# Chunk attention and a token mixer on one core: two heads on alternate partitions, pair-writing transposes, three v buffers and another order

## The chip, the cores and the metric

The kernel runs on one core of a Trainium2 chip. The metric is device time in microseconds (us) from one launch; the runs before the change took 118.61 to 119.23 us, median 118.85. The engines are TensorE (PE, with its weight loads as PEld), VectorE (DVE), ScalarE (ACT), GpSimd (POOL) and SyncE (SP). Each engine runs its own instructions in order and waits on semaphores for the others.

## The reference

Two steps follow each other. First an attention in which each chunk of 64 tokens sees only itself; then a mixer over all 576 tokens of a batch. There are 8 batches, 8 heads, 576 tokens (9 chunks of 64) and 64 values per head.

```
scores = q_c @ k_c^T / sqrt(64)            # per batch, head, chunk: 64 x 64
attn   = exp(scores - max) / sum           # softmax over the chunk
x      = attn @ v_c                        # then heads side by side: [8, 576, 512]
W      = (x @ w_q) @ (x @ w_k)^T / sqrt(64)   # 576 x 576 per batch
out    = relu(W @ x) @ w_out               # [8, 576, 512], float32
```

The inputs are float32 and the output is float32. The kernel works in f16 with float32 sums in PSUM.

## The kernel before, in words

The whole program is one list of words, ORDER (lines 18 to 51). Each word is one step of one batch, and the loop at line 404 emits the steps in that order, so the list fixes the order of the instructions on every engine. `SC3.1@4` is a step SC of batch 3, part 1, into PSUM bank 4; `:A`, `:D` or `:P` at the end of a word says whether ScalarE, VectorE or GpSimd does it. A word that issues DMAs or has no letter has a fixed engine. The words, in the order in which a batch needs them:

- LD (`load`, line 115): a DMA issued by GpSimd that also turns float32 into f16. k and q come in two halves, `LD3.k0` and `LD3.k1`, each half holding four heads; v comes in four parts. Of v only half is loaded, in rows of two tokens; CP (`pair`, line 144) copies it within vt so that each row holds both members of a pair. vt has NVB = 4 buffers (line 81), used by batch number modulo 4, so a v load waits for the PV of four batches before.
- TR (`tr`, line 172): VectorE transposes 32 x 32 blocks of qk, seen as pairs of f16 in one float32, into kN or qT. One instruction covers one half (four heads) of k or of q: 576 elements in each partition. Each element is written 36 bytes (kN) or 72 bytes (qT) after the one before.
- MK (`mk`, line 182): copies kN into kT times a mask of zeros and ones, so that two heads that share a matmul don't mix. One word is two instructions, for even and for odd chunks.
- SC (`sc`, line 192): score matmuls on TensorE, 64 x 64 each, two at a time in the two halves of the rows. EX (line 206): the exponential, PSUM to SBUF, ScalarE. PV (line 220): attn times v, with a column of ones that gives the sum. RN (line 251): reciprocal and division on VectorE, into xn.
- XT, XE (lines 262, 270): transposing xn on TensorE and copying it out of PSUM. PJ, EP (lines 277, 299): the projection by w_q and w_k, copied into wqk. DU (line 302) copies half of it to the other partitions. WT, EW (lines 305, 313): the transposed w_k side. GM, EG (lines 320, 334): the product of w_k side and xn, 64 x 512, copied into g16. So W @ x is never formed from W; w_q side times g16 (MX, line 337) gives it. RL (line 349): relu, into rmx.
- OM, OE (lines 374, 386): the output projection for 128 rows, four matmuls of 512 columns, and its copy out of PSUM into the qk tile of that pair of batches, which is free by then. There are 36 of them. When a group of OE is complete, SyncE stores it. The first two stores are made to wait for the last two loads (line 476).
- ZZ (line 400): a dummy matmul of 512 columns on zeros, whose result nobody reads. There are 48, 41 of them before the first EP.

Other single words: CL (ones in vt), CZ (zeros in zz and wqk), MM (the mask), ID (identity), WS and WO (the weights).

GpSimd does the load issues and most CP and some DU words in one queue. A CP waits until its part of v has landed, and the loads behind it in the list wait with it.

The last lines of ORDER before, from the EP of batch 7 on, show how the end is built: eight output projections stand behind it.

```
MX6.0@0 OM24@6 RL6.0:A XT7.0@0 XT7.1@4 MX6.2@2 OM25@1 RL6.2:A XE7.0:D XE7.1:D PJ7@4 OM28@0 OE25:A EP7:A WT7@1 OM27@4
EW7:D GM7@1 OM29@5 OE29:D DU7:P OE28:A OE26:A OE24:A EG7:A OE27:A MX7.0@0 MX7.1@6 MX7.2@2 RL7.1:A RL7.0:D OM30@4
RL7.2:A MX7.3@6 RL7.3:A OE30:D OM31@0 OE31:D OM32@6 OM34@7 OM33@0 OE32:D OE34:A OE33:D OM35@7 OE35:A
```

Of the kernel before, what the change touches and what calls it, by code (L numbers as in the profile page):

```python
# [18 lines left out]
CZ ZZ@0 LD0.k0 MM ZZ@1 ZZ@2 ZZ@3 ZZ@4 ZZ@5 ZZ@6 ZZ@7 CL0 TR0.1 CL2 CL1 ZZ@0 ZZ@1 ZZ@2 LD0.q0 LD0.k1 LD0.q1 LD0.v1  # L19
LD0.v0 LD0.v2 LD0.v3 LD1.q0 LD1.v1 LD1.k0 ID WS LD2.q0 CP0.3:P LD1.k1 LD1.q1 CP1.1:P LD1.v0 LD1.v2 LD2.k0 LD1.v3 WO  # L20
LD2.v1 LD2.k1 CP1.0:P CP1.2:P LD2.v0 LD2.q1 CP1.3:P LD2.v2 LD2.v3 LD3.q0 TR0.0 TR0.3 MK0.3:D TR0.2 CP0.1:D CP0.2:D
MK0.0:A MK0.1:A MK0.2:A ZZ@3 ZZ@4 ZZ@5 ZZ@6 ZZ@7 ZZ@0 ZZ@1 SC0.0@0 ZZ@2 ZZ@3 ZZ@4 ZZ@5 ZZ@6 ZZ@7 SC0.2@6 SC0.1@4 EX0.0
CP0.0:A EX0.2 EX0.1 ZZ@2 PV0.0@2 ZZ@0 PV0.1@4 PV0.2@0 ZZ@6 ZZ@7 ZZ@6 ZZ@7 ZZ@6 RN0.0 RN0.1 ZZ@2 ZZ@3 ZZ@7 XT0.0@7 ZZ@6
XE0.0:A RN0.2 XT0.1@0 XE0.1:A ZZ@4 ZZ@5 ZZ@2 ZZ@3 ZZ@6 ZZ@4 PJ0@0 EP0:A TR1.1 TR1.0 MK1.0:D MK1.1:D SC1.0@4 WT0@0
EX1.0 TR1.3 EW0:D TR2.0 CL3 DU0:D TR1.2 MK1.2:A GM0@0 ZZ@7 ZZ@2 PV1.0@2 RN1.0 EG0:A MX0.2@0 MX0.3@6 MK1.3:A RL0.2:A
RL0.3:A TR2.1 MK2.1:D SC1.1@4 EX1.1 SC1.2@0 MX0.0@6 RL0.0:A ZZ@2 ZZ@3 ZZ@2 MX0.1@2 EX1.2 RL0.1:A PV1.1@4 PV1.2@0 ZZ@6
RN1.1 MK2.0:A OM1@6 XT1.0@7 RN1.2 OM2@4 XT1.1@0 XE1.0:D TR2.3 MK2.2:D MK2.3:D TR2.2 LD3.k0 LD3.k1 CP2.0:P LD3.v0
LD3.v1 LD4.k0 CP2.2:P LD3.q1 LD3.v2 LD4.k1 LD3.v3 CP3.0:P CP3.1:P LD4.v0 LD4.q1 LD4.q0 LD5.k0 CP3.2:P LD4.v2 LD4.v1
CP3.3:P SC2.0@2 OM0@7 OE1:A CP2.1:A XE1.1:A EX2.0 OE2:A PJ1@0 PV2.0@2 RN2.0 CP2.3:D TR3.0 EP1:A WT1@6 SC2.1@0 SC2.2@4
DU1:A EW1:A EX2.1 GM1@6 PV2.1@0 RN2.1 EX2.2 EG1:A OE0:A MX1.0@4 MX1.1@2 RL1.0:A RL1.1:A MX1.3@6 PV2.2@4 MX1.2@0  # L30
RL1.3:A RL1.2:A TR3.1 RN2.2 OM4@2 OM6@3 XT2.0@0 MK3.0:A XT2.1@4 TR3.3 MK3.1:D MK3.3:D MK3.2:D TR4.1 ZZ@6 TR3.2 OM5@1
SC3.0@6 OE4:A XE2.0:A XE2.1:A OE5:A EX3.0 PJ2@4 EP2:A OE6:A OM8@1 WT2@0 SC3.1@4 SC3.2@2 OE8:A EW2:A EX3.1 PV3.0@6
EX3.2 GM2@0 PV3.1@4 EG2:A MK4.1:A MK4.0:D TR4.3 RN3.0 OM7@2 OE7:A RN3.1 DU2:P LD5.q0 CP4.0:P LD4.v3 PV3.2@6 MX2.2@0
RL2.2:A MX2.1@4 RL2.1:A MK4.2:D RN3.2 TR4.0 MK4.3:D TR5.1 TR4.2 XT3.0@3 XE3.0:A MX2.0@0 OM3@2 RL2.0:A MX2.3@6 RL2.3:A
XT3.1@4 XE3.1:A LD5.q1 LD5.v1 LD5.k1 LD6.q0 LD5.v3 CP4.1:P CP4.2:P LD5.v0 CP4.3:P LD5.v2 CP5.1:P LD6.k0 LD6.v1 LD6.v3
LD6.k1 LD7.v0 LD6.v2 LD6.q1 LD6.v0 CP5.0:P CP5.2:P CP5.3:P LD7.k0 SC4.0@0 OM9@3 PJ3@4 EX4.0 OE9:A EP3:A OE3:A PV4.0@0
SC4.1@6 EX4.1 WT3@4 OM10@5 SC4.2@2 EW3:A EX4.2 MK5.0:D TR5.0 DU3:D RN4.0 PV4.1@6 RN4.1 GM3@4 PV4.2@0 RN4.2 OM11@2
MK5.1:A EG3:A OE10:A MX3.0@6 MX3.1@3 XT4.0@5 OE11:A RL3.0:A RL3.1:A XT4.1@0 SC5.0@6 MX3.2@2 TR5.3 XE4.0:D MK5.3:D
MK5.2:D TR5.2 XE4.1:A OM13@4 RL3.2:A EX5.0 PJ4@0 MX3.3@2 OM12@5 EP4:A RL3.3:A OE13:A OE12:A SC5.1@0 EX5.1 SC5.2@2
WT4@4 PV5.0@6 EX5.2 EW4:A TR6.0 TR6.1 RN5.0 OM16@5 PV5.1@0 RN5.1 PV5.2@2 GM4@4 RN5.2 OM15@6 XT5.0@7 OE16:A MK6.0:A  # L40
EG4:A MK6.1:D TR6.3 XE5.0:D TR6.2 MK6.3:D MK6.2:D TR7.1 LD7.k1 CP6.1:P LD7.q0 DU4:P LD7.v2 CP7.0:P LD7.v3 CP6.0:P
CP6.3:P LD7.q1 LD7.v1 CP6.2:P MX4.3@4 MX4.1@0 OE15:A RL4.3:A RL4.1:A XT5.1@2 XE5.1:A SC6.0@4 MX4.2@0 OM17@6 EX6.0
PJ5@2 OM14@7 MX4.0@4 OE17:A EP5:A RL4.2:A RL4.0:A WT5@6 EW5:D SC6.1@2 EX6.1 PV6.0@0 SC6.2@4 EX6.2 RN6.0 GM5@6 PV6.1@2
PV6.2@4 RN6.1 RN6.2 DU5:P EG5:A OE14:A MX5.0@0 OM19@6 OM20@7 MK7.1:A RL5.0:A OE19:A OE20:A XT6.0@2 XE6.0:A XT6.1@4
MX5.1@0 RL5.1:A MX5.2@6 TR7.3 XE6.1:D OM18@3 PJ6@4 MK7.3:A EP6:A RL5.2:A OM23@2 TR7.0 MK7.0:D SC7.0@0 WT6@4 MX5.3@6
OE18:A EW6:A CP7.2:P CP7.3:P CP7.1:P DU6:P TR7.2 OE23:D RL5.3:D MK7.2:D EX7.0 OM21@5 GM6@4 PV7.0@0 SC7.2@6 SC7.1@2
OE21:A EG6:A EX7.2 EX7.1 RN7.0 MX6.1@4 OM22@6 RL6.1:D MX6.3@0 PV7.1@2 PV7.2@4 RN7.1 RN7.2 RL6.3:A OE22:A OM26@7
MX6.0@0 OM24@6 RL6.0:A XT7.0@0 XT7.1@4 MX6.2@2 OM25@1 RL6.2:A XE7.0:D XE7.1:D PJ7@4 OM28@0 OE25:A EP7:A WT7@1 OM27@4
# [6 lines left out]
def kernel(  # L55
# [87 lines left out]

    def pair(b, half, f, eng):
        m = slice(NG // 2 * half, NG // 2 * (half + 1))
# [24 lines left out]
            )  # L170

    def tr(b, g, s):
        to = (kN if s else qT[b % 2])[:, g].bitcast(F32).rearrange("p n o -> p (n o)")
# [6 lines left out]
        nc.vector.transpose(out=to, in_=frm)  # L180

    def mk(b, g, hp, eng):
        one = mask[:, hp : hp + 1]
        for odd in range(2):
            dst = kT[b % 2][:, g, odd::2, hp ^ odd].rearrange("p c (e i) o -> p c e (i o)", e=2)
            frm = kN[:, g].rearrange("p (e c i) o -> p c e (i o)", e=2, c=NCH)[:, odd::2]
            if eng == "A":
                nc.scalar.activation(dst, frm, AF.Copy, scale=one)  # L188
            else:
                nc.vector.tensor_scalar(dst, frm, one, None, op0=ALU.mult)  # L190

    def sc(b, u, bank):
        for i in range(8 if u < 2 else 2):
            g, c = (u, i) if u < 2 else (i, NCH - 1)
            for e in range(2):
                for t in range(2):
                    rows = slice(CH * t, CH * t + CH)
                    nc.tensor.matmul(  # L198
                        ps[:, bank + t, CH * i : CH * i + CH],
                        lhsT=kT[b % 2][rows, g, c, :, :, e].rearrange("p f n -> p (f n)"),  # L200
                        rhs=qT[b % 2][rows, g, CH * c : CH * c + CH, e],
                        start=(e == 0),
                        stop=(e == 1),
                    )
# [199 lines left out]
    for word in ORDER:  # L404
# [17 lines left out]
        elif kind == "CZ":  # L422
            nc.vector.memset(zz[:].bitcast(F32), 0.0)  # L423
# [88 lines left out]
```

## Time and profile before

| | |
|---|---|
| median of 3 runs | 118.85 us (118.61 to 119.23) |
| the profiled execution, its own time | 118.47 us |
| its span, first to last instruction | 116.6 us |
| TensorE clock granted, mean | 0.985 of full |
| busy: PE, DVE, ACT, POOL | 99.8, 92.4, 89.5, 61.9 us |
| loads (GpSimd's queue), written | 14.82 MB |
| stores (SyncE's queue) | 9.44 MB |

All durations come from one execution, whose span is 116.6 us. A row of the slices gives for each fortieth of the span (2.9 us) the busy share of an engine in tenths, where 9 means 90% or more. In the groups, a row names line, engine, operation, what is written from what, the shape and the count, then the busy time in us and the mean of one in ns, then the idle time of the engine just ahead of such instructions and what ended it. In the view by windows a row is one stretch of time with the busy time of each engine in it and the number of its instructions. The chain of work that ended last follows the end of the span back to what released each step.

### The profile page before, as it was taken

The numbers are of one execution on the slowest core, as the hardware profiler recorded it, in microseconds if no ns is written. First come the engines' busy times: TensorE is split into PE (matmuls) and PEld (weight loads), VectorE is DVE, ScalarE is ACT, GpSimd is POOL, SyncE is SP. The second block draws the span as 40 slices with busy tenths as digits, with TensorE's granted clock in tenths as the row PEclk, the third lists the DMA queues.
The fourth block names the chain that finished last, engine by engine and source line by source line (L and its number), as shares of the span: only waits on it lengthen the run. The fifth ranks groups of instructions, "written<-read, shape, count | busy, mean of one in ns | idle before, by whom it ended". The sixth has DMA issues, their size and how long they took to land.

```text
span 116.6 us, 4132 instructions
## 1 busy us (share of the span) xinstructions
PE 99.8 (86%) x1768; PEld 55.9 (48%) x1768; DVE 92.4 (79%) x155; ACT 89.5 (77%) x142; POOL 61.9 (53%) x105
## 2 busy tenths in 40 slices
...
DVE  2099399999999999999997999998799768515520
...
PEclk9999599999999999999999999999999999999999
DMA  1999999999999999999999999999799986007982
GB/s 11 177 200 177 199 194 211 192 201 203 197 193 204 196 201 186 190 195 194 189 195 165 169 178 200 210 192 129 296 400 415 411 351 280 23 3 304 379 315 88
DMA packets 27202, 24.52 MB, mean 210 GB/s; under 512 B 20784, under 2 KB 20784, under 8 KB 27184
## 3 DMA queue, kind: packets, MB, share of 16 engines
q0 software_dynamic: 24880, 14.82, 90.8%
q1 hardware_dynamic: 2304, 9.44, 20.3%
q8 instruction: 14, 0.23, 0.7%
...
HBM read 29.62 MB, written 9.44 MB: 335 GB/s over the span
## 4 chain that ended last, share of the span: by engine, by line
DMA 43%; PE 33%; POOL 12%; issue 5%; ACT 2%; DVE 1%; POOLq 0%; DVEq 0%
DMA vt<-in_v_dram 39%; PE pb L378 18%; POOL vt L295 6%; DMA qk<-in_q_dram 4%; POOL vt L122 3%; POOL qk L138 3%; PE pb L341 3%; PE pb L198 3%; PE pb L283 3%; PE pb L266 3%; PE pb L325 2%; PE pb L232 2%; ACT qk L293 1%; DVE xn L255 1%; ACT rmx L356 1%
## 5 line engine op out<-in xcount | busy, mean ns | idle before, releaser
L378 PE MATMUL pb<-wout,rmx 128*128 128x512 f16 x144 | 36.4, 382 | 0.0
L255 DVE TENSOR_TENSOR xn<-pb,rec 128x896 f16<-128x896 f32 (+1 forms) x24 | 25.1, 1047 | 0.8
L295 POOL COPY vt<-vt 32x576 int32<-32x576 int32 x27 | 18.1, 674 | 11.4 <-DMA vt<-in_v_dram 10.7
L122 POOL DMA_DIRECT2D vt<-in_v_dram x32 | 21.8, 687 | 3.4 <-DMA vt<-in_v_dram 1.2
L356 ACT ACTIVATE rmx<-pb 128x576 f16<-128x576 f32 x29 | 18.3, 663 | 5.9 <-PE pb L341 5.7
L180 DVE STREAM_TRANSPOSE kN<-qk 128x576 f32<-128x576 f32 x16 | 19.4, 1213 | 4.0 <-DMA qk<-in_k_dram 4.0
L188 ACT ACTIVATE kT<-kN,mask 128x640 f16<-128x640 f16 (+1 forms) x24 | 17.4, 786 | 5.1 <-DVE kN L180 4.9
L293 ACT COPY qk<-pb 128x512 f32<-128x512 f32 x30 | 17.6, 607 | 4.1 <-PE pb L378 3.9
L180 DVE STREAM_TRANSPOSE qT<-qk 128x576 f32<-128x576 f32 x16 | 19.7, 1243 | 0.1
L208 ACT ACTIVATE est<-pb 128x1024 f16<-128x1024 f32 (+1 forms) x24 | 19.2, 826 | 0.4 <-PE pb L198 0.3
L378 PEld LDWEIGHTS <-rmx 128*128 128x128 f16 x144 | 12.5, 103 | 13.0 <-issue 0.5
L198 PE MATMUL pb<-qT,kT 64*128 64x64 f16 x576 | 13.0, 193 | 4.0 <-ACT kT L188 2.8
L401 PE MATMUL pb<-zz 128*128 128x512 f16 x48 | 14.5, 437 | 1.2 <-DVE zz L423 1.2
L190 DVE TENSOR_SCALAR kT<-kN,mask 128x640 f16<-128x640 f16 (+1 forms) x40 | 14.9, 423 | 0.1
L198 PEld LDWEIGHTS <-kT 64*128 64x128 f16 x576 | 10.8, 96 | 8.1 <-ACT kT L188 4.2
L293 ACT COPY xT<-pb 128x1280 f16<-128x1280 f16 (+1 forms) x10 | 11.4, 1146 | 4.0 <-PE pb L266 3.7
L295 POOL COPY wq<-wqk 64x288 int32<-64x288 int32 x5 | 2.1, 422 | 22.6 <-ACT wqk L293 19.1
L232 PE MATMUL pb<-vt,est 64*64 64x65 f16 x576 | 9.9, 197 | 2.4 <-issue 1.8
L266 PE MATMUL pb<-ident,xn 128*128 128x128 f16 (+1 forms) x160 | 10.9, 214 | 0.4 <-DVE xn L255 0.4
L266 PEld LDWEIGHTS <-xn 128*128 128x128 f16 (+1 forms) x160 | 9.2, 97 | 3.9 <-issue 1.2
L232 PEld LDWEIGHTS <-est 64*64 64x64 f16 x576 | 7.8, 109 | 6.4 <-issue 5.0
L138 POOL DMA_DIRECT2D qk<-in_k_dram x16 | 9.2, 576 | 2.5 <-DMA qk<-in_k_dram 1.1
...
## 6 DMA issues: line engine op xcount, KB each, us to landing
...
qk<-in_k_dram POOLq DMA_DIRECT2D x16, 288.0 KB, 8.0
qk<-in_q_dram POOLq DMA_DIRECT2D x16, 288.0 KB, 7.9
vt<-in_v_dram POOLq DMA_DIRECT2D x32, 144.0 KB, 7.8
...
```

The lines of the kernel that those rows point to most:

```text
L122: nc.gpsimd.dma_start(vt[b % NVB][CH * f + 32 : CH * f + CH, m, 0 : 2 * D], src[:, NG * half + f : NG * (half + 1) : 2],)
L180: nc.vector.transpose(out=to, in_=frm)
L188: nc.scalar.activation(dst, frm, AF.Copy, scale=one)
L198: nc.tensor.matmul(ps[:, bank + t, CH * i : CH * i + CH], lhsT=kT[b % 2][rows, g, c, :, :, e].rearrange("p f n -> p (f n)"), rhs=qT[b % 2] ...
L208: nc.scalar.activation(est[b % 2][u].rearrange("p i n c -> p i (n c)"), ps[:, bank : bank + 2, 0:n], AF.Exp, scale=scale_attn,)
L232: nc.tensor.matmul(ps[CH * o : CH * o + CH, bank + hp, VP * m : VP * m + VP], lhsT=est[b % 2][t][rows, i, at], rhs=vt[b % NVB][rows, slot, ...
L255: nc.vector.tensor_tensor(out=xn[b % 2][:, 7 * u : 7 * u + n].rearrange("p m (h d) -> p h m d", h=2), in0=xw[:, :, :, 0:D], in1=rec[u][:, ...
L266: nc.tensor.transpose(t16[:, at % 1024 : at % 1024 + r], xn[b % 2][0:r, n, :], ident[0:r, 0:r])
L293: nc.scalar.copy(dst, src)
L295: nc.gpsimd.tensor_copy(dst.bitcast(I32), src.bitcast(I32))
L356: nc.scalar.activation(dst, src, AF.Relu, scale=scale_moe)
L378: nc.tensor.matmul(ps[:, bank, :], lhsT=c.rearrange("p (t r) -> p r t", r=size)[:, r], rhs=wout[:, i, :], start=(i == 0), stop=(i == NI - 1),)
```

## The change

The two transposes of a batch's halves become one, for batches 1 to 7. Batch 0 keeps the old layout. For the others, a load of one half puts its 64 rows on every other partition, so that the two halves alternate from partition to partition; one row is 9216 bytes in memory, 36 tokens, where it was 4608 bytes. A transpose of all 128 partitions then finds the two halves side by side in each 32 x 32 block, and writes them side by side: two float32 of 4 bytes in a row, then a step. One TR instruction has 1152 elements.

The tiles follow: in kT and qT the two halves alternate element by element (8 bytes from one to the next of a half, as SC reads them), kN and kT get a tenth, empty chunk so that even and odd chunks fit one pattern, and one MK word is one instruction. For batches 1 to 7 one MK does 2560 elements and there are two a batch instead of four. The words TRn.4 and TRn.5 are the joint transposes of q and of k, MKn.4 and MKn.5 the joint copies.

vt has three buffers, not four. GM's last step reads all 128 rows instead of 64 (the added ones are zero on one side). A memset clears the empty part of kN once.

ORDER is another list as a whole, 462 words instead of 537:

| words | before | after |
|---|---|---|
| ZZ | 48 | 2 |
| TR | 32 | 18 |
| MK on ACT, on DVE | 12, 20 | 7, 11 |
| CP on ACT, DVE, POOL | 2, 3, 27 | 2, 12, 18 |
| RL on ACT, DVE | 29, 3 | 24, 8 |
| XE on ACT, DVE | 10, 6 | 8, 8 |
| OE on ACT, DVE | 30, 6 | 29, 7 |
| EP on ACT, DVE | 8, 0 | 6, 2 |
| DU on ACT, DVE, POOL | 1, 2, 5 | 2, 4, 2 |

The diff, cut to its core:

```
-    NVB = 4
+    NVB = 3
...
-    qT = [sb.tile([P, 2, S, 2], F16, name=f"qT{i}") for i in range(2)]
-    kN = sb.tile([P, 2, S, 2], F16, name="kN")
-    kT = [sb.tile([P, 2, NCH, 2, CH, 2], F16, name=f"kT{i}") for i in range(2)]
+    qT = [sb.tile([P, 2 * S, 2], F16, name=f"qT{i}") for i in range(2)]
+    SP = S + CH
+    kN = sb.tile([P, 2 * SP, 2], F16, name="kN")
+    kT = [sb.tile([P, 4 * SP, 2], F16, name=f"kT{i}") for i in range(2)]
...
     def load(b, what):
...
+        src = (q, k)[s][b]
+        if b == 0:
+            dst = qk[0][:, 0, s, RUN * n : RUN * n + RUN]
+            src = src.rearrange("(g h) (p r) d -> g (h p) (r d)", g=2, r=RUN)[n]
+        else:
+            dst = qk[b // 2][n::2, b % 2, s]
+            src = src.rearrange("(g h) (p r) d -> g (h p) (r d)", g=2, r=NG)[n]
+        loads.append(nc.gpsimd.dma_start(dst.rearrange("p r d -> p (r d)"), src))
...
     def tr(b, g, s):
...
+        elif s:
+            to = to.rearrange("p (e n) -> p e n", e=2)[:, :, 0:S]
+            to = to.rearrange("p e (x r g) -> p r e x g", r=RUN, g=2)
+            frm = frm.rearrange("p (r e) (x g) -> p r e x g", e=2, g=2)
+        else:
+            to = to.rearrange("p (x r g) -> p r x g", r=NG, g=2)
+            frm = frm.rearrange("p r (x g) -> p r x g", g=2)
         nc.vector.transpose(out=to, in_=frm)

     def mk(b, g, hp, eng):
...
+        dst = dst.rearrange("p (m j e i) o -> p m j e (i o)", j=4, e=2, i=n)
+        dst = dst[:, :, 1:3] if hp else dst[:, :, 0::3]
+        frm = frm.rearrange("p (e m j i) o -> p m j e (i o)", e=2, j=2, i=n)
...
     def sc(b, u, bank):
+        if b == 0:
+            qv = qT[0].rearrange("p (g n) o -> p g n o", g=2)
+            kv = kT[0].rearrange("p (g c m) o -> p g c m o", g=2, c=NCH + 1)
+        else:
+            qv = qT[b % 2].rearrange("p (n g) o -> p g n o", g=2)
+            kv = kT[b % 2].rearrange("p (c m g) o -> p g c m o", c=NCH + 1, g=2)
...
-                        lhsT=kT[b % 2][rows, g, c, :, :, e].rearrange("p f n -> p (f n)"),
-                        rhs=qT[b % 2][rows, g, CH * c : CH * c + CH, e],
+                        lhsT=kv[rows, g, c, :, e],
+                        rhs=qv[rows, g, CH * c : CH * c + CH, e],
...
     def gm(b, bank):
-                r = P if j < 4 else CH
-                    lhsT=wkn[b % 2][0:r, j, :],
-                    rhs=xn[b % 2][0:r, n, :],
+                    lhsT=wkn[b % 2][:, j, :],
+                    rhs=xn[b % 2][:, n, :],
```

Of the new ORDER, its start up to the EP of batch 1, and the stretch around the EP of batch 3:

```
CZ LD0.k1 CL0 MM TR0.3 CL1 CL2 LD0.k0 LD0.q1 LD0.q0 LD0.v1 ID LD0.v2 LD0.v0 LD0.v3 LD1.v1 LD1.k0 WS LD1.k1 LD1.q1
LD1.q0 LD1.v0 LD1.v3 LD1.v2 LD2.k0 LD2.k1 WO CP1.1:P LD2.q0 LD2.q1 LD2.v1 CP1.0:P LD2.v0 CP1.2:P CP1.3:P TR0.1 MK0.0:D
TR0.2 TR0.0 CP0.1:D CP0.0:D CP0.2:D CP0.3:D MK0.2:A MK0.3:A MK0.1:A SC0.1@0 SC0.0@2 SC0.2@4 EX0.1 EX0.0 EX0.2 PV0.0@2
PV0.2@4 RN0.2 PV0.1@0 RN0.1 RN0.0 TR1.5 ZZ@6 XT0.1@0 XE0.1:A XT0.0@2 ZZ@7 XE0.0:D MK1.5:D TR1.4 PJ0@2 MK1.4:A SC1.0@0
EX1.0 SC1.1@6 PV1.0@0 EX1.1 EP0:D LD2.v3 LD2.v2 RN1.0 SC1.2@2 EX1.2 WT0@4 EW0:A DU0:A PV1.1@6 GM0@4 PV1.2@0 EG0:A
RN1.1 RN1.2 MX0.3@4 MX0.0@2 RL0.3:A MX0.1@6 MX0.2@4 RL0.0:A RL0.1:A RL0.2:A XT1.0@0 XE1.0:A XT1.1@6 XE1.1:A TR2.5
OM2@4 OM1@5 OE2:A CP2.1:A OE1:A MK2.4:D MK2.5:D PJ1@6 TR2.4 EP1:D SC2.0@0 SC2.1@2 WT1@6 OM0@7 CP2.0:D DU1:D EW1:D
...
SC4.1@2 PV4.0@4 TR5.5 RN4.0 XE3.1:A EX4.2 EX4.1 PJ3@0 PV4.2@2 PV4.1@6 RN4.1 EP3:A WT3@0 OM9@1 EW3:A GM3@0 OE9:A EG3:A
LD6.k0 DU3:P LD5.v0 LD5.v1 LD5.v3 LD6.q1 LD5.v2 LD7.k1 LD7.k0 LD6.v1 LD7.q0 CP5.1:P LD6.v0 CP5.3:P LD7.q1 LD6.v3
LD6.v2 LD7.v1 CP6.1:P LD7.v3 CP6.0:P LD7.v0 CP6.3:P LD7.v2 CP6.2:P XT4.0@6 MX3.1@0 MX3.0@4 RN4.2 MK5.4:D RL3.0:D
MK5.5:D TR5.4 TR6.5 CP5.0:D XE4.0:A RL3.1:A XT4.1@2 XE4.1:A MX3.3@6 MX3.2@0 RL3.3:A RL3.2:A OM14@4 PJ4@2 OE14:A EP4:A
```

More of the change, by code (lines that the diff above doesn't have):

```diff
@@ L18 @@
 ORDER = """
[L19 to L48, printed above, removed]
@@ new lines @@
+PV0.2@4 RN0.2 PV0.1@0 RN0.1 RN0.0 TR1.5 ZZ@6 XT0.1@0 XE0.1:A XT0.0@2 ZZ@7 XE0.0:D MK1.5:D TR1.4 PJ0@2 MK1.4:A SC1.0@0
+EX1.0 SC1.1@6 PV1.0@0 EX1.1 EP0:D LD2.v3 LD2.v2 RN1.0 SC1.2@2 EX1.2 WT0@4 EW0:A DU0:A PV1.1@6 GM0@4 PV1.2@0 EG0:A
+RN1.1 RN1.2 MX0.3@4 MX0.0@2 RL0.3:A MX0.1@6 MX0.2@4 RL0.0:A RL0.1:A RL0.2:A XT1.0@0 XE1.0:A XT1.1@6 XE1.1:A TR2.5
+OM2@4 OM1@5 OE2:A CP2.1:A OE1:A MK2.4:D MK2.5:D PJ1@6 TR2.4 EP1:D SC2.0@0 SC2.1@2 WT1@6 OM0@7 CP2.0:D DU1:D EW1:D
+CP2.3:D CP2.2:D LD3.q0 LD3.k1 LD3.k0 LD4.k1 LD3.q1 LD4.k0 LD3.v0 LD3.v1 LD3.v2 LD3.v3 LD4.q1 LD4.q0 LD4.v1 LD5.k1
@@ new lines @@
+CP3.2:P LD4.v0 LD4.v2 LD5.k0 LD4.v3 EX2.0 EX2.1 PV2.0@0 RN2.0 GM1@6 PV2.1@2 SC2.2@4 RN2.1 OE0:A EG1:A EX2.2 MX1.0@6
+RL1.0:A MX1.1@0 RL1.1:A PV2.2@4 MX1.3@6 MX1.2@0 RL1.3:A RL1.2:A RN2.2 TR3.5 XT2.0@2 OM5@3 XE2.0:A OE5:A MK3.5:A
+XT2.1@4 XE2.1:D MK3.4:D TR3.4 OM3@2 PJ2@4 OM6@3 EP2:A OE6:A OE3:A LD6.k1 CP4.1:P CP4.0:P LD5.q1 LD6.q0 CP4.2:P CP4.3:P
+LD5.q0 SC3.0@0 WT2@4 EW2:A SC3.1@6 SC3.2@2 EX3.0 EX3.2 EX3.1 GM2@4 OM7@5 TR4.5 DU2:D CP3.0:D EG2:D CP3.1:D CP3.3:D
+MX2.2@2 RL2.2:A PV3.0@0 RN3.0 MK4.5:D MX2.3@6 MX2.1@2 RL2.3:A OE7:A RL2.1:A OM4@4 MX2.0@6 RL2.0:A PV3.2@0 PV3.1@2
@@ L51 @@
+OM35@4 OE35:A
 """.split()
```

57 lines of the change are left out of this document (28 added, 29 removed).

## The prediction

> **What bounds the kernel now.** I read the page first: the span, the busy shares and the slices.
>
> ```profile
> span 116.6 us, 4132 instructions
> PE 99.8 (86%) x1768; PEld 55.9 (48%) x1768; DVE 92.4 (79%) x155; ACT 89.5 (77%) x142; POOL 61.9 (53%) x105
> ...
> DVE  2099399999999999999997999998799768515520
> ...
> PEclk9999599999999999999999999999999999999999
> DMA  1999999999999999999999999999799986007982
> ```
>
> No engine is busy all the time, but from slice 7 on one of them always is. So I cut the span where each batch's projection leaves PSUM (the word EP, one CAST into wqk). The second and the eighth are these, with the last copy to an output row, from the timeline:
>
> ```profile
> 35.33 0.67 ACT L293 CAST wqk<-pb 128x576 f16<-128x576 f32 x1
> ...
> 102.24 0.64 ACT L293 CAST wqk<-pb 128x576 f16<-128x576 f32 x1 [0.44 <-PE pb L283]
> ...
> 112.14 0.59 ACT L293 COPY qk<-pb 128x512 f32<-128x512 f32 x1 [1.14 <-PE pb L378]
> ```
>
> The view by windows, cut at the EPs (columns: stretch, its length, then busy time of PE, PEld, DVE, ACT, POOL, the granted clock, DMA, GB/s):
>
> ```profile
> 5.70:21.70 16.00, 12.80 (x210) 6.82 (x210) 13.55 (x23) 9.74 (x13) 11.65 (x20) 0.89 1.38 195
> 21.70:35.30 13.60, 11.86 (x263) 7.07 (x262) 13.03 (x22) 13.42 (x20) 8.87 (x15) 1.00 1.40 199
> 35.30:46.80 11.50, 10.08 (x212) 6.17 (x209) 11.33 (x19) 11.31 (x20) 8.00 (x13) 1.00 1.37 196
> 46.80:57.90 11.10, 10.43 (x237) 6.07 (x239) 11.00 (x18) 10.96 (x20) 8.78 (x15) 1.00 1.34 192
> 57.90:67.90 10.00, 8.96 (x209) 5.51 (x197) 9.20 (x16) 9.07 (x16) 8.57 (x14) 1.00 1.38 178
> 67.90:80.10 12.20, 10.07 (x215) 6.08 (x214) 12.10 (x20) 10.06 (x18) 8.18 (x14) 1.00 1.36 196
> 80.10:89.60 9.50, 9.45 (x184) 5.81 (x183) 8.32 (x14) 9.37 (x17) 2.39 (x4) 1.00 0.88 317
> 89.60:102.20 12.60, 11.76 (x223) 6.57 (x222) 8.76 (x14) 8.25 (x15) 0.42 (x1) 1.00 0.68 272
> 102.20:112.70 10.50, 9.91 (x59) 4.04 (x57) 4.45 (x7) 6.05 (x11) 0.42 (x1) 1.00 0.64 249
> ```
>
> From EP1 to EP6 (35.3 to 89.6, 54.3 us) the busiest engine of each stretch adds up to 11.33 + 11.00 + 9.20 + 12.10 + 9.45 = 53.1 us, 98%. VectorE and ScalarE hold it until 80 us, TensorE after that. So the time is nearly the sum, stage by stage, of the busiest engine's work. Loads run at about 195 GB/s as written (the row counts the halved f16 side) until 80 us and never gate a whole stage.
>
> **The change part by part.** Prices, from the groups with shapes kept apart:
>
> ```profile
> L255 DVE TENSOR_TENSOR xn<-pb,rec 128x896 f16<-128x896 f32 x16 | 17.5, 1092 | 0.6
> L254 DVE RECIPROCAL rec<-pb 128x14 f32<-128x14 f32 x16 | 3.6, 223 | 4.9 <-PE pb L232 4.7 <-ACT est L208 0.2
> L180 DVE STREAM_TRANSPOSE qT<-qk 128x576 f32<-128x576 f32 x16 | 19.7, 1243 | 0.1
> L180 DVE STREAM_TRANSPOSE kN<-qk 128x576 f32<-128x576 f32 x16 | 19.4, 1213 | 4.0 <-DMA qk<-in_k_dram 4.0
> L190 DVE TENSOR_SCALAR kT<-kN,mask 128x640 f16<-128x640 f16 x20 | 8.8, 441 | 0.1
> L190 DVE TENSOR_SCALAR kT<-kN,mask 128x512 f16<-128x512 f16 x20 | 8.1, 406 | 0.0
> L188 ACT ACTIVATE kT<-kN,mask 128x640 f16<-128x640 f16 x12 | 10.1, 844 | 5.1 <-DVE kN L180 4.9
> L188 ACT ACTIVATE kT<-kN,mask 128x512 f16<-128x512 f16 x12 | 8.7, 727 | 0.0
> L358 DVE TENSOR_SCALAR rmx<-pb 128x576 f16<-128x576 f32 x3 | 2.3, 751 | 0.1
> L356 ACT ACTIVATE rmx<-pb 128x576 f16<-128x576 f32 x29 | 18.3, 663 | 5.9 <-PE pb L341 5.7
> L297 DVE COPY vt<-vt 32x1152 f16<-32x1152 f16 x3 | 1.4, 453 | 0.7 <-DMA vt<-in_v_dram 0.6
> L297 DVE COPY qk<-pb 128x512 f32<-128x512 f32 x6 | 4.1, 689 | 4.1 <-PE pb L378 4.1
> L297 DVE COPY xT<-pb 128x1280 f16<-128x1280 f16 x2 | 1.6, 812 | 0.0
> L401 PE MATMUL pb<-zz 128*128 128x512 f16 x48 | 14.5, 437 | 1.2 <-DVE zz L423 1.2
> L423 DVE MEMSET zz<- 128x256 f32 x1 | 0.3, 272 | 0.9 <-PEq L496 0.9
> ```
>
> *Transposes (TR).* Batches 1 to 7 had 28 instructions of 576 elements, 28 x 1.228 = 34.4 us; they get 14 of 1152. No row shows one that writes pairs. Upper end: the price follows elements, 2 x 1.243 = 2.49 us each, nothing saved. Lower end: one element per step, as the dense memset does (256 in 272 ns), 1152 x 1.06 = 1.22 us. Today an element costs 2.1 ns, twice the memset's, and each lands alone, 36 bytes (kN) or 72 (qT) from the last. The rows differ, 1213 against 1243 ns, with nothing but that step different, so the write side has a say in the price. I take a price per *separate place written*: still 576 places, 1.23 us, 14 x 1.23 = 17.2 us, 17.2 saved. It is the largest guess here.
>
> *Masked copies (MK).* A group costs two instructions now, 0.441 + 0.406 on VectorE or 0.844 + 0.727 on ScalarE. The slope between the rows (128 elements: 35 ns and 117 ns) gives 0.97 and 2.60 us for the new form of 2560 elements, which replaces two groups. VectorE: 20 x 0.847 = 16.9 becomes 10 x 0.97 + 0.6 = 10.3. ScalarE: 12 x 1.571 = 18.9 becomes 4 x 2.60 + 3 x 1.43 = 14.7.
>
> *Work handed to VectorE by the new order.* RL 3 to 8 (+3.8 us), v copies 3 to 12 (+4.1), OE 6 to 7 (+0.7), XE +2 of the wide form (+1.6), EP, EG, DU and EW +2.0 net by the rows of their like. ScalarE loses five RL (3.3), two wide XE, two EP; GpSimd loses nine v copies. Net in instruction time: VectorE -17.2 - 6.6 + 12.2 = -11.6 us, ScalarE about -11.
>
> *By stage.* I counted the words of each ORDER between two EPs, times these prices, less what neighbours overlap (0.06 us an instruction on VectorE, 0.09 on ScalarE, which makes before's totals 93.1 and 88.5 against the page's 92.4 and 89.5), with PE at the rate of the chain's rows further down (20 matmuls, five OM, in 4.44 us; an MX in 0.23). The heaviest stage after, EP2 to EP3, on VectorE: 3 TR 3.7, 1 MK 0.9, 5 RN 5.9, 3 v copies 1.2, 2 OE 1.3, XE, DU and EG 1.1: 14.1 us. The rest, busiest engine of each:
>
> - before, EP1 to the end: 11.3, 11.3, 10.1, 12.3, 9.7, 12.0, 8.6: 75.3 us, where the trace took 112.7 - 35.3 = 77.4 (97%).
> - after: 9.8, 14.1, 6.4, 13.1, 8.4, 9.4, 9.4: 70.6 us; at the same 97% 72.6 us.
>
> That is 4.8 us off. TensorE's own work is nearly unchanged (one OM and one MX fewer after EP6) and it becomes as loaded as the two others, about 47 us each from EP1 to EP6; this is why 11 us less on two engines brings less than half of it.
>
> *Start.* The first transpose stays where it was:
>
> ```profile
> 5.69 1.21 DVE L180 STREAM_TRANSPOSE kN<-qk 128x576 f32<-128x576 f32 x1 [3.80 <-DMA qk<-in_k_dram]
> ```
>
> EP1 in the new order, following ScalarE: its three MK from 7 us on, then EX, XE, MK1.4, three EX, EW, DU, EG, four RL and two XE run nearly without a gap to 33.4, PJ1 takes one more: 34.5, against 35.3. But 46 of 48 dummy matmuls (437 ns each) go, which filled TensorE's gaps there. The clock row has one slice at 5 even with them. Between nothing and, with all the matmuls of that chain (my count of PE rows there, some 8 us) at half rate, 8 us; I take 0.8, because ScalarE and not TensorE is the chain: EP1 stays at 35.3.
>
> *Three v buffers.* LD3 to LD7 of v wait for PV of three batches before, not four; in the order each stands behind that anyway. What is new is DU3 on GpSimd ahead of LD5's v: GpSimd's queue stands until EP3 (about 59), and all of v5, q and k of 7 and v6, v7 are queued behind it.
>
> ```profile
> vt<-in_v_dram POOLq DMA_DIRECT2D x32, 144.0 KB, 7.8
> qk<-in_k_dram POOLq DMA_DIRECT2D x16, 288.0 KB, 8.0
> ```
>
> Issued at 60, v5 lands near 67, and VectorE gets to its copy CP5.0 some 5 us after EP3, near 65: a wait of 0 to 3 us, in a light stage; I take 0.7. q and k loads move the same bytes in half as many, twice as long runs: nothing, hidden as loads are until 80 us.
>
> *Matmuls of SC* read both operands 8 bytes apart, not 4.
>
> ```profile
> 77.37 0.52 PE pb L198 x32
> ...
> 107.45 0.23 PE pb L341 x2
> 107.68 4.44 PE pb L378 x20
> ```
>
> From the chain that ended last (start, length, what): 32 take 0.52 us. Between nothing and double (504 x 16 ns = 8 us on TensorE, some 3 of it on the path); I take nothing, since at 4 bytes two row halves together already go at 16 ns each. The 64 further rows of GM's last step and the padding memset cost under 0.1 us.
>
> *Sum.* 35.3 + 72.6 + 0.7 = 108.6 for the last copy; from it to the end before took 116.6 - 112.7 = 3.9: span 112.5. The profiled execution took 118.47, 1.87 more than its span: 114.4. The median of the runs is 118.85, 0.4 above: **114.8 us**, its own range 112 to 117.5.
>
> The Trainium skill, page "SBUF — State Buffer", section "Specifications (TRN2)", says that memory lines are 16 bytes and that two hits in a line are needed for full rate; by it pairs of 4 bytes go at full rate, and the sum is the one above. The rows (2.1 ns for lone writes, 1.06 for dense ones) agree so far, and none shows a pair.
>
> **The rivals.**
>
> *The transpose is paid by the element* (slower). Then a TR of 1152 costs 2.44 us. For it: all 32 transposes have the same 2.1 ns, at steps that differ by a factor of two. Against it: the memset's 1.06. VectorE's stages become 11.7, 17.7, 8.9, 13.1 (ScalarE), 9.6, so the sum is 79.8, not 70.6; with 97% 9.5 us more, and TR1.5 and TR1.4 in the chain to EP1 2.4 more, of which other engines' slack takes some 2: about 124.6 (121 to 128). It decides from where the gain of 4 us is eaten: 9.2 + 2.4 us per 1.21 us of price, so above some 1.65 us for one instruction.
>
> The Trainium skill, page "VectorE: DVE Perf Modes", section "The three transpose paths", gives 311 ns for a 128x128 bf16 transpose, 2.4 ns an element. By that rule writing pairs saves nothing, and the time is this rival's. Our 1243 ns for 576 is the same slope.
>
> *Start or loads* (about even). TensorE stays at half clock to 30 us, or GpSimd's stand at DU3 lets the loads dry up and v5 and v7 come 3 us late. Either moves an EP by 3 to 5 us: 118 to 119.5. For it: the clock's slice at 5; DMA at 9 in every slice, so no reserve to catch up. Against: ScalarE carries the start.
>
> *SC at half rate:* 117 to 118.
>
> *Better:* the three nearly equal engines interlock as well as VectorE did before (98%) and the start reaches 34: 109.5 to 112.
>
> **How the numbers follow.** Forecast 0.44, better 0.11, SC 0.05, start or loads 0.14, price by the element 0.26. Two runs 0.5% apart are about what can be told from no change. Start or loads I share as 0.05, 0.05 and 0.04. Faster: 0.44 + 0.11 + 0.05 + 0.05 = 0.65; same 0.05; slower 0.04 + 0.26 = 0.30. The range goes down to 110, and up to 125, half of the transpose rival.
>
> **What would show it.** The TR rows: 128x1152 near 1.23 us or near 2.44. MK near 0.97 and 2.60 us. EP1 at 35.3, EP3 near 59, EP6 near 87; DVE busy near 82 us (99 in the rival), ACT near 80, POOL near 54. A copy of v5 that keeps VectorE idle under 1 us. It is wrong if a clock row of 5 lasts beyond slice 8, or if from EP1 on no engine is busy over 90% of a stage: then waits, not work, set the time.

## The result, and the profile after

The changed kernel takes 164.89 us (164.19 to 165.81, 4 runs), the kernel before in the same comparison 118.73 (118.37 to 119.23, 4 runs). The ratio is 1.389, interval 1.380 to 1.398. The forecast was 114.8 with a range of 110 to 125: wrong in sign, and by 50 us. The profiled execution took 165.81 us, of which the span is 164.0. Some launches of a kernel are 1.5% or more longer than its fastest one; the times and ratios below leave them out.

From the page of after: span, busy time, and three rows of slices (here a slice is 4.1 us).

```profile
span 164.0 us, 3988 instructions
...
PE 103.1 (63%) x1722; PEld 63.2 (39%) x1722; DVE 93.7 (57%) x133; ACT 82.9 (51%) x116; POOL 54.9 (33%) x93
...
DVE  1300096994997809000089899500799889676550
...
PEclk9999999999999998795557999996559999999998
DMA  3999999930006999998900009999989805305495
```

The engines did hardly more work than before; they stood. The transfers, busy in nearly every slice before, have two stretches of three or four empty slices and are thin at the end. A full row of DMA had been my reason to cost the loads at nothing. By stage, cut again at the EPs (length, then busy PE, PEld, DVE, ACT, POOL, clock, DMA, GB/s):

```profile
36.50:49.50 13.00, 12.52 (x211) 8.50 (x212) 10.03 (x12) 9.99 (x15) 0.00 (x0) 1.00 0.01 3
49.50:64.90 15.40, 10.94 (x211) 7.25 (x210) 10.14 (x16) 9.69 (x13) 8.58 (x14) 0.98 1.12 169
64.90:96.60 31.70, 17.67 (x333) 10.76 (x333) 14.63 (x21) 13.99 (x21) 8.46 (x14) 0.74 0.61 98
...
104.00:131.60 27.60, 17.35 (x295) 11.05 (x296) 15.45 (x18) 13.55 (x21) 10.17 (x16) 0.81 1.11 239
```

The busiest engine fills 71%, 56% and 63% of the last three. In the first, TensorE still has work, but GpSimd issues nothing for 13 us and 3 GB/s arrive. Both signs that the prediction named for its own failure are there: stages in which no engine is over 90% busy, so waits set the time, and a clock row of 5 beyond slice 8. EP1, EP3 and EP6 fall at 49.5, 96.6 and 140.4, not at 35.3, 59 and 87.

Which waits, by the view of waits (total us, times, longest):

```profile
DVE kN L187 <- DMA qk<-in_q_dram: 33.6, 3, 16.0
PE pb L215 <- DVE qT L187: 25.3, 3, 23.9
POOL qk L136 <- DVE qT L187: 23.0, 1, 23.0
```

The first row is odd: a transpose of *k* into kN waits for loads of *q*. The third is odder: GpSimd, about to issue a load, waits for a transpose. The timelines show both (start, length, what, idle time before and its releaser); the first three rows are VectorE's, the last GpSimd's.

```profile
5.68 1.20 DVE L187 STREAM_TRANSPOSE kN<-qk 128x576 f32<-128x576 f32 x1 [3.75 <-DMA qk<-in_k_dram]
...
20.55 1.20 DVE L187 STREAM_TRANSPOSE kN<-qk 128x576 f32<-128x576 f32 x1 [13.35 <-DMA qk<-in_q_dram]
...
81.96 1.38 DVE L187 STREAM_TRANSPOSE kN<-qk 128x1152 f32<-128x1152 f32 x1 [15.96 <-DMA qk<-in_q_dram]
```

```profile
49.56 0.55 POOL L136 DMA_DIRECT2D qk<-in_q_dram  x1 [22.98 <-DVE qT L187]
```

The first transpose goes at 5.7 us as forecast. The second (TR0.1) reads batch 0's k, issued second of all loads, and goes only at 20.6. The load at 49.56 is LD3.q0, batch 3's q; it stood 23 us, until TR2.4, batch 2's transpose of q, was through, and every later load stood behind it in GpSimd's queue. Batches 2 and 3 share one qk tile, as 0 and 1 do.

The program as built says it outright. These are some of its waits, in short form (DMASW0 to 7 are the eight semaphores that GpSimd's loads take in turn; qk_63 is the tile of batches 0 and 1):

```
VectorE  TR0.3  kN<-qk_63             [waits DMASW0]
         TR0.1  kN<-qk_63             [waits DMASW5, DMASW6, DMASW4, DMASW1]
GpSimd   LD1.k0 qk_63<-in_k_dram      [waits DMASW1, DVE]
         LD3.q0 qk_64<-in_q_dram      [waits DMASW3, DVE]
```

TR0.1 needs one load, LD0.k0. It waits for all four of batch 1's: LD1.k1, LD1.q1 and LD1.q0 on semaphores 4, 5 and 6, and LD1.k0, the second load on semaphore 1. **Theory A**: a load whose destination is every second partition (`[n::2]`) is tracked as one that touches the whole tile. So whatever reads or writes another part of that tile is put in order with it, in both directions: transposes behind the loads of the other batch, loads behind the transposes of the other batch. The rivals: **B**, the new order with three v buffers starves VectorE by itself; **C**, transfers to alternate partitions are slow.

### The profile page after: what moved, and what is told of

It is laid out like the page before. It is cut to its first block, busy times and chain, and to the rows that moved or that the text cites. A ratio compares the mean times of both kernels' runs of the same rounds, so it can differ in the third digit from the quotient of the medians.

```text
span 164.0 us, 3988 instructions
## 1 busy us (share of the span) xinstructions
PE 103.1 (63%) x1722; PEld 63.2 (39%) x1722; DVE 93.7 (57%) x133; ACT 82.9 (51%) x116; POOL 54.9 (33%) x93
## 4 chain that ended last, share of the span: by engine, by line
PE 36%; issue 5%; DVE 5%; DMA 3%; ACT 2%; DVEq 0%
PE pb L394 17%; PE pb L215 6%; DMA qk<-in_q_dram 3%; PE pb L283 3%; PE pb L249 3%; PE pb L300 2%; PE pb L357 2%; PE pb L341 2%; DVE kT L201 2%; DVE xn L272 1%; DVE qT L187 1%; ACT qk L310 1%; ACT est L225 1%; PE pb L326 0%; ACT wq L310 0%
## 5 line engine op out<-in xcount | busy, mean ns | idle before, releaser
L187 DVE STREAM_TRANSPOSE kN<-qk 128x1152 f32<-128x1152 f32 (+1 forms) x9 | 12.0, 1335 | 48.5 <-DMA qk<-in_q_dram 33.6
L215 PE MATMUL pb<-qT,kT 64*128 64x64 f16 x576 | 20.5, 238 | 25.3 <-DVE qT L187 25.3
L215 PEld LDWEIGHTS <-kT 64*128 64x128 f16 x576 | 18.2, 117 | 27.8 <-issue 15.0
L199 ACT ACTIVATE kT<-kN,mask 128x2560 f16<-128x2560 f16 (+1 forms) x7 | 13.7, 1967 | 21.3 <-DVE kN L187 21.3
L357 PE MATMUL pb<-wqk,g 64*128 64x288 f16 x32 | 8.3, 318 | 15.0 <-DVE g L314 14.0
L136 POOL DMA_DIRECT2D qk<-in_q_dram x16 | 8.8, 551 | 25.9 <-DVE qT L187 23.0
L201 DVE TENSOR_SCALAR kT<-kN,mask 128x2560 f16<-128x2560 f16 (+1 forms) x11 | 16.1, 1477 | 0.1
L312 POOL COPY vt<-vt 32x576 int32<-32x576 int32 x18 | 12.1, 675 | 8.8 <-DMA vt<-in_v_dram 8.4
L300 PE MATMUL pb<-xT,wpj 128*128 128x512 f16 x64 | 10.2, 307 | 4.3 <-DVE xT L314 4.0
L187 DVE STREAM_TRANSPOSE qT<-qk 128x1152 f32<-128x1152 f32 (+1 forms) x9 | 11.9, 1342 | 0.0
(43 smaller groups left out, 105.4 us busy)
```

What stands on the lines that cost most here:

```text
L215: nc.tensor.matmul(ps[:, bank + t, CH * i : CH * i + CH], lhsT=kv[rows, g, c, :, e], rhs=qv[rows, g, CH * c : CH * c + CH, e], start=(e == 0),
```

## Experiments

**e1_halves_apart.** One line: the two halves go to the lower and the upper 64 partitions. The heads are then paired wrongly; counts and shapes stay.

```diff
-            dst = qk[b // 2][n::2, b % 2, s]
+            dst = qk[b // 2][64 * n : 64 * n + 64, b % 2, s]
```

> The changed kernel, but each load of half of q or k writes 64 neighbouring partitions (0 to 63 or 64 to 127) and not every other one; nothing else differs, so the scores are those of wrongly paired heads. Theory A (a write to every other partition counts as touching the whole qk tile, so that transposes wait for the loads of the other batch in the tile and loads wait for its transposes): the waits of kN's transposes on q's loads (33.6 us) and of GpSimd on qT's transposes (23 us) go, and the time falls to 117 to 121 us: my sum of 114.8 with the prices now measured, 1.37 us a joint transpose (not 1.23) and 1.54 a VectorE copy MK (not 0.97), 3 to 4 us more. Rival B (the new order or the third v buffer holds the loads back by itself): DMA still idles for three long stretches, 145 us or more. Rival C (the rows on every other partition land more slowly): also fast here, so the second run decides.

**e2_own_tiles.** Alternate partitions stay; each batch has a tile for q and one for k, so that there is nothing else in the tile to wait for. This is the changed kernel's whole computation.

```diff
-    qk = [sb.tile([P, 2, 2, NG, D], F16, name=f"qk{i}") for i in range(B // 2)]
+    qk = [[sb.tile([P, NG, D], F16, name=f"qk{i}_{s}") for s in range(2)] for i in range(B)]
+    ox = [sb.tile([P, DM], F32, name=f"ox{i}") for i in range(B // 2)]
...
-    GROUPS = [[3, 3, 3], [3, 3, 3], [3, 3, 3], [3, 1, 1, 1, 1, 1, 1]]
+    GROUPS = [[2, 2, 2, 2, 1], [2, 2, 2, 2, 1], [2, 2, 2, 2, 1], [2, 1, 1, 1, 1, 1, 1, 1]]
```

> The changed kernel with rows on every other partition kept, but q and k of each batch in tiles of their own, so that no two batches share one; the output rows are staged two to a tile (stores of 512 KB instead of 768 KB, and one single row a pair). Same order, same three v buffers, the whole computation. Theory A: no transpose waits for another batch, 117 to 121 us, the same as the run before within 2 us. Rival B: 145 us or more, as unchanged as the order. Rival C (slow rows): the run before fast and this one at 140 or more, with the q and k loads at over 10 us from issue to landing.

**e3_old_order.** As e2, but with the order of before (a joint TR or MK at the place of the first half that it replaces, TR5.5 and TR7.5 later), four v buffers and two ox tiles instead of four. Of its edit only the line on the buffers is shown.

```diff
-    NVB = 3
+    NVB = 4
```

> The new layout, the joint transposes and joint copies, own tiles as in the run above, but the order of the kernel before with its 48 dummy matmuls and four v buffers; the joint words stand where the first of the two halves stood. The order was made for halves, so a joint transpose waits for the later of two loads. Theory A: no stop of over 5 us on any engine; VectorE has some 15 us less to do than before (transposes 34.4 to 19.2 us, copies 16.9 to 15 or less), but a joint transpose at the place of the first half comes too early: 114 to 120 us. If the new layout itself is the loss, over 125 us.

Measured, beside the kernel before at 117.69 us: e1 123.28 (one run), e2 122.75 (two runs, 122.72 and 122.78), e3 145.33 (144.34 to 145.60, ratio 1.234, interval 1.225 to 1.244). e1 and e2 take away some 42 us, by two edits that share only this: the false waits are gone. In the programs as built, TR0.1 waits for DMASW1 alone in both, and LD3.q0 no longer waits for VectorE. Both times lie some 2 us above the 117 to 121 expected. From the page of e2:

```profile
span 121.0 us, 4005 instructions
...
PE 97.2 (80%) x1722; PEld 60.4 (50%) x1722; DVE 94.3 (78%) x133; ACT 82.4 (68%) x116; POOL 54.2 (45%) x93
...
DMA  1999999999999999999960899999999994860874
```

DVE's work is the same as in after, 94.3 against 93.7 us; 43 us of standing are gone. C falls: in e2 transfers still go to alternate partitions, and loads of q and k take about as long from issue to landing (medians 8.1 and 7.9 us, in after 7.2 and 7.7, in the kernel before 7.9 and 8.0). B falls as the cause of the 42 us, as e1 and e2 keep the order and the three buffers. e3 missed its 114 to 120 us. It has no false waits, but with a joint transpose at the first half's place VectorE waits 19.4 us before transposes for q and k loads (4.0 in the kernel before), and is busy for only 80.4 of 143.4 us. So the pair layout doesn't suit the old order; what makes up the rest of e3's 28 us was not traced.

**e8_before_halves and e9_before_alternate.** The same cause in the kernel *before*, where there are no pairs, no new order and four buffers. Each q and k load is given as two:

```diff
+        for a in range(2):
+            rows = slice(64 * a, 64 * a + 64)      # e8
+            rows = slice(a, 128, 2)                # e9
...
+            loads.append(nc.gpsimd.dma_start(dst[rows], frm[rows]))
```

> The kernel before, with each of its q and k loads given as two of 64 partitions, the lower and the upper half. The control of the next run: twice as many q and k transfers are issued on GpSimd, nothing else. All theories: between the kernel before and some 5% above it, with waits for loads of the same kind as before.

> The same two transfers for each load, but each fills every second partition (0, 2, 4 and 1, 3, 5). Bytes, number of transfers, tiles, transposes and order are those of the run before; only which partitions a transfer names differs. Theory A (a write to alternate partitions is tracked as one to the whole tile, so transposes and loads of the two batches and of q and k that share a tile wait for each other): 135 us or more, 15 to 50% above the run before, with long idle stretches of the transfers and of VectorE before transposes, and with no pair-writing, no new order and three buffers to blame. If the cost lies in pair-writing, in the order or in the buffers: within 2% of the run before. If transfers to alternate partitions are themselves slow (theory C): above the run before, but with the transfers busy in nearly every slice.

Measured beside 116.06 us (3 runs): e8 121.2 (ratio 1.043, interval 1.032 to 1.053), e9 172.28 (1.485, 1.473 to 1.498). The page's rows of DMA, e8 first, then e9, and the two longest waits of e9 at a load:

```profile
DMA  2999999999999999999999999999979999506982
```

```profile
DMA  4199999997000699992436999910049999950594
```

```profile
POOL qk L138 <- DVE qT L176: 23.8, 2, 19.0
POOL qk L138 <- DVE kN L176: 20.1, 2, 15.7
```

The same bytes in as many transfers, and 51 us apart: only the step of the partitions differs. A single load is not slower by it (medians of k and q from issue to landing: 5.4 and 5.1 us in e8, 4.9 and 5.1 in e9). The programs as built differ in their waits:

```
VectorE  TR0.0 in e8   qT<-qk_63      [waits DMASW3, DMASW2]
         TR0.0 in e9   qT<-qk_63      [waits DMASW5, DMASW4, DMASW6, DMASW3, DMASW7, DMASW2, DMASW0]
```

The two semaphores of e8 are those of the two transfers that fill this half of q. Together with e1 and e2 this shows theory A. What the tracking does inside was not looked at; the waits that it writes into the program were.

**What is left over the kernel before.** e2 is still 5 us above it. The groups of e2 (busy us, mean ns of one) name two prices that I had wrong:

```profile
L216 PE MATMUL pb<-qT,kT 64*128 64x64 f16 x576 | 20.4, 238 | 13.5 <-DVE qT L188 13.1 <-DVE xn L273 0.4
L216 PEld LDWEIGHTS <-kT 64*128 64x128 f16 x576 | 18.4, 116 | 15.5 <-ACT kT L200 10.3 <-issue 4.7 <-DVE kT L202 0.2
L202 DVE TENSOR_SCALAR kT<-kN,mask 128x2560 f16<-128x2560 f16 x10 | 15.2, 1538 | 0.1
L200 ACT ACTIVATE kT<-kN,mask 128x2560 f16<-128x2560 f16 x4 | 9.7, 2424 | 0.0
L188 DVE STREAM_TRANSPOSE qT<-qk 128x1152 f32<-128x1152 f32 x7 | 9.6, 1371 | 0.0
L188 DVE STREAM_TRANSPOSE kN<-qk 128x1152 f32<-128x1152 f32 x7 | 9.5, 1361 | 0.0
```

SC's matmuls were 13.0 us (193 ns) and their weight loads 10.8 before. Four kernels, from e2 (e4, e5 and e7 multiply wrong pairs of rows):

```diff
 # e4: both operands 4 bytes apart; e5: only qv
-            qv = qT[b % 2].rearrange("p (n g) o -> p g n o", g=2)
+            qv = qT[b % 2].rearrange("p (g n) o -> p g n o", g=2)
-            kv = kT[b % 2].rearrange("p (c m g) o -> p g c m o", c=NCH + 1, g=2)
+            kv = kT[b % 2].rearrange("p (g c m) o -> p g c m o", g=2, c=NCH + 1)
 # e6: MK on VectorE in two; e7: e4 and e6
-            nc.vector.tensor_scalar(dst, frm, one, None, op0=ALU.mult)
+            for j in range(2):
+                nc.vector.tensor_scalar(dst[:, :, j], frm[:, :, j], one, None, op0=ALU.mult)
```

> The kernel with own tiles, its score matmuls reading both operands 4 bytes apart, as batch 0 does already, for all batches (it multiplies wrong pairs of rows, so the scores are of no use; counts, shapes and order are unchanged). If the 8-byte step is what still separates the kernel with own tiles from its forecast (theory S): the score matmuls' busy time falls from 20.4 to about 13 us and their weight loads' from 18.4 to about 11, and the time falls by 3 to 4.5 us, to 119 to 121, because TensorE is busy all the time in the last three stages before the last projection. If masked copies or the order hold the rest (theories M and O): the rows fall all the same, the time by under 1 us.

> As the run before, but only q is read 4 bytes apart, k stays at 8. If the moving operand (q) sets the price, the matmul rows fall to 13 us and the weight loads stay at 18; if the weights (k) set it, both rows stay near 20 and 18. By theory S with both operands at fault, the time falls by 1 to 2.5 us.

> The kernel with own tiles, each masked copy on VectorE given as two instructions of half the elements, with one loop fewer in each pattern; the same elements are copied. Theory M1 (the loop too many takes VectorE out of its fast rate): each of the two takes 0.45 to 0.6 us for 1280 elements, so that ten of them save some 4 us on VectorE and the time falls by 1.5 to 3 us. Theory M2 (the place where the pieces lie, or the length of the run, sets the rate): the two take 0.88 us each, 1.76 for the pair, and the time rises by about 1 us.

> Score matmuls at 4-byte steps and VectorE's masked copies split, together. If both are what is missing (S and M1): 115 to 118 us, below the kernel before. If the order or the three v buffers hold the rest (O): above 120.

Measured beside 117.56 us (18 runs): e4 117.55 (ratio 1.000, interval 0.996 to 1.004), e5 118.31 (1.007, 1.003 to 1.011), e6 122.06 (1.040, 1.034 to 1.047), e7 115.54 (0.985, 0.978 to 0.992). SC's rows in e4, then in e5, and the copies of e6:

```profile
L212 PE MATMUL pb<-qT,kT 64*128 64x64 f16 x576 | 13.2, 199 | 14.1 <-DVE qT L188 13.1 <-issue 0.5 <-DVE xn L269 0.4
L212 PEld LDWEIGHTS <-kT 64*128 64x128 f16 x576 | 11.8, 100 | 16.6 <-ACT kT L200 10.3 <-issue 6.0
```

```profile
L215 PE MATMUL pb<-qT,kT 64*128 64x64 f16 x576 | 13.4, 200 | 13.9 <-DVE qT L188 13.5 <-DVE xn L272 0.4
L215 PEld LDWEIGHTS <-kT 64*128 64x128 f16 x576 | 12.4, 115 | 15.9 <-ACT kT L200 10.7 <-issue 4.7 <-DVE kT L202 0.2
```

```profile
L203 DVE TENSOR_SCALAR kT<-kN,mask 128x1280 f16<-128x1280 f16 x20 | 12.2, 659 | 0.1
```

e4 gained 5.2 us on e2, more than the 3 to 4.5 expected. The moving operand q holds most of the price: with q at 4 bytes and k still at 8, the busy times of both rows are nearly back. e5 missed its expectation (1 to 2.5 us, and the weight loads staying at 18): it gained 4.4 of e4's 5.2. A weight load is no shorter in e5 than in e2 (115 and 116 ns; 100 in e4), so the 18.4 us of e2 seem to be loads spread out beside slow matmuls.

e6 missed too: it gained 0.7 us on e2, less than the scatter of its own runs (121.45 to 123.07), not 1.5 to 3. Two copies of 1280 take 1.32 us where one of 2560 took 1.54, between the 0.9 to 1.2 of theory M1 and the 1.76 of M2. That the loop too many is the cause isn't shown. In the programs as built, the source of either copy has three loops; what differs is its outermost count, 10 against the destination's 5 in the copy of 2560 and in batch 0's of 1280 (879 ns), 5 against 5 in the split copies (659 ns). No run separates this from the length of the pieces. With q near, the same split gains 2.0 us (e4 to e7).

**e10_q_lone, e11_q_lone_late, e12_all_lone.** From e6, with the whole computation kept: q is loaded and transposed as before and read 4 bytes apart (e10: batches 1 to 7, e11: 5 to 7), and in e12 k too, with its shorter copies.

```diff
-        if b == 0:
+        if b == 0 or s == 0:
...
-            to = to.rearrange("p (x r g) -> p r x g", r=NG, g=2)
-            frm = frm.rearrange("p r (x g) -> p r x g", g=2)
+            for i in range(2):
+                nc.vector.transpose(
+                    out=to[:, S * i : S * i + S].rearrange("p (x r) -> p r x", r=RUN),
+                    in_=frm[:, RUN * i : RUN * i + RUN],
+                )
```

> The kernel with own tiles and split masked copies, with q loaded and transposed as before (two column halves, lone writes, two instructions of 576), so that the score matmuls read q 4 bytes apart; k stays pair-written. The whole computation. TensorE gets back some 7 us, VectorE pays 7 x (2.48 - 1.37) = 7.8 us. If VectorE is the bound where it is full (batches 1 to 4): 118 to 121 us, between the run with split copies (122.1) and the one with both (116.2). If VectorE has room: 116 to 118, level with or below the kernel before.

> The same with q so only for batches 5 to 7, whose score matmuls run where TensorE was busy all the time (73 to 108 us of the kernel with own tiles), and pair-written for 1 to 4. TensorE gets 3 x 0.9 = 2.8 us back there, VectorE pays 3 x 1.1. If TensorE alone is the bound there: 119 to 120. If VectorE is level with it: 121 to 122.5, no gain.

> The kernel with own tiles, new order and three v buffers, but with k too loaded, transposed (two instructions of 576), copied (four VectorE pieces of 640, or two ScalarE pieces of 1280, for a word of batch 1 to 7) and read as batch 0 is. No pairs are left; the whole computation. VectorE: 96.4 of the run with lone q, + 7 x 1.1 for transposes, + 10 x 0.4 for shorter copies: 108 us. If the new order is the cause of what is left over the kernel before, because it hands VectorE work that only the pairs would pay for: 125 to 130 us. If the order costs nothing and pairs gain nothing: 118 to 120.

Measured: e10 119.90 (1.034, interval 1.026 to 1.041), e11 120.55 (1.038, 1.031 to 1.045), both beside 116.06, and e12 128.5 (1.094, 1.087 to 1.100) beside 117.37. Busy time in e10, then in e12:

```profile
PE 93.2 (78%) x1722; PEld 54.9 (46%) x1722; DVE 96.4 (81%) x151; ACT 82.4 (69%) x116; POOL 55.4 (46%) x93
```

```profile
PE 95.1 (75%) x1722; PEld 55.9 (44%) x1722; DVE 105.4 (83%) x178; ACT 83.5 (66%) x120; POOL 56.1 (44%) x93
```

Pairing q costs: e6 is 2.2 us slower than e10, though VectorE has 5.5 us less to do there (90.9 in e6). Pairing k, with the longer copies that it allows, gains 8.6 us (e10 against e12). And e12 puts a price on the new order with its three buffers: without pairs the kernel is 11 us slower than before. VectorE has 13 us more to do than before (105.4 against 92.4), and only the pairs pay for that; the order and the buffers were not tried apart. e11 lies between e6 and e10, 0.65 us above e10 with ranges that overlap; it doesn't tell the late stages from the early ones. No version with the whole computation came below the kernel before.

## Why the prediction was wrong, by its steps

**The step that failed** is the one that reads "q and k loads move the same bytes in half as many, twice as long runs: nothing, hidden as loads are until 80 us", with the one that loads "never gate a whole stage". The bytes did cost nothing. The waits cost some 42 us (164.9 to 122.75 in e2, 123.3 in e1). I counted bytes, run lengths and places in GpSimd's queue, but not what each load and each transpose waits for in the program as built, and the list of those waits was there to be read: TR0.1 with four semaphores instead of one. No rival of mine had it either; "start or loads" thought of 3 to 5 us.

**TR.** The disputed price came out on the side I took, and "paid by the element" fell: 1371 and 1361 ns for 1152 elements, not 2.44 us. Mine was 1.23, so 14 x 0.14 = 2 us too little. The Trainium skill, page "SBUF — State Buffer", section "Specifications (TRN2)", asks for two hits in a 16-byte line for full rate. Pairs of 4 bytes at 1.19 ns an element, where lone writes took 2.1, agree with it. The 2.4 ns an element that the rival worked out from the Trainium skill's page "VectorE: DVE Perf Modes", section "The three transpose paths", is twice what a pair-writing transpose cost here; the page does not say how its transpose writes.

**MK.** The slope of two rows did not carry to the new form: 1.54 us for 2560 elements on VectorE, not 0.97. That is 5.7 us more work. Split in two, which takes back part of it, it is worth 0.7 us of time in e6 and 2.0 in e7. On ScalarE 2.42, below my 2.60.

**SC.** Mis-sized. I took nothing and gave a doubled rate a chance of 0.05 and "some 3" us on the path. Measured: 7.4 us more on TensorE, nearly the upper bound of 8, and 5.2 us of time (e2 to e4). The share on the path was wrong because I had TensorE at about 47 us from EP1 to EP6, as loaded as the two others. In e2 it is busy for 57.2 of the 61.2 us between them, and fills the late stages:

```profile
73.40:88.40 15.00, 15.00 (x294) 9.96 (x291) 14.06 (x17) 13.19 (x19) 8.38 (x14) 1.00 1.32 184
88.40:97.20 8.80, 8.80 (x189) 5.49 (x191) 7.83 (x12) 6.83 (x11) 1.72 (x3) 1.00 1.02 397
97.20:107.60 10.40, 10.40 (x179) 6.19 (x177) 7.74 (x13) 6.23 (x12) 0.00 (x0) 1.00 0.76 297
```

The Trainium skill's rule on 16-byte lines (the page named above) doesn't extend here: at 8 bytes two f16 of a moving operand also share a line, and the matmuls were slower all the same (238 against 199 ns). The measurement decides.

**VectorE's busy time.** 93.7 us, not near 82. The transposes saved 15.2 us instead of 17.2 and the copies on VectorE 0.8 instead of 6.6; the instructions also overlap by 0.03 us each, not the 0.06 that I took (in after counts times means of its groups add up to 98.2 us).

**Right:** VectorE's 12.2 us of added work (12.2 by the rows of after too). The start: without false waits EP1 is at 36.0 in e2, 34.2 in e7, and the clock holds about as well without the dummy matmuls (0.986 over the span of e2, 0.985 in the kernel before). Three buffers and DU3: in e2 the DMA row shows the stand (a slice at 0), and VectorE waits 0.9 us for v in all, where I took 0.7. ACT and POOL busy: 82.9 and 54.9 for "near 80" and "near 54".

**The sum.** With the false waits gone and SC and MK nearer the prices that I took, e7 gives 115.54 us, 2.0 below the kernel before in the same comparison (117.56); the forecast was 4.0 below its own 118.85. So half of the forecast gain is there; but e7, like e4, multiplies wrong pairs of rows, and with q in pairs and the rows kept right SC has to read q at 8 bytes. What holds the other half was not measured apart: e7's VectorE still has 14 x 0.14 us of TR and 10 x 0.35 of MK (1.32 against 0.97) more than the sum took.
